# A fused attention and expert kernel: a second buffer for weight conversion, slopes read as rows, block 2's scores behind block 1's transposes, each weight scaling in its own slot

## The chip, the cores and the metric

The kernel runs on one core of a Trainium2 chip. The metric is the time of one execution in device microseconds (us); less is better.

## What is computed

Three stages follow one another. The middle one has the weights that most of the change is about.

```python
# attention: 4 x 8 heads, 576 positions, window of 128, a bias by distance
scores = q @ k.T / sqrt(64) + bias, masked to 0 <= rel < 128
x = softmax(scores) @ v                       # 2304 tokens x 512
# dense layer: w_in 512 x 2048, w_out 2048 x 512, alpha 2048
h = x @ w_in
y = (max(h, 0) + alpha * min(h, 0)) @ w_out
# experts: logits = y @ w_gate; 288 tokens go to each of 8 experts
out[mask] = max(y[mask] @ w1[e], 0) @ w2[e]
```

## The kernel before

The 2304 tokens are 18 blocks of 128. The 8 heads are done in halves, so attention has 36 steps n (block n // 2, half n % 2). The dense layer goes over 9 units u of two blocks and 16 slices f of the hidden dimension: 144 **slots** (u, f), numbered 16 u + f. Slot (u, f) is `l1` (TensorE: `ph`; then two or three operations that make `g`) and, one slot later, `l2` (TensorE: `py`).

`w_in` and `w_out` come as 64-bit numbers, in 16 tiles of 1 MB, one per f. `load_w64` fetches one into `raw` (four buffers), and `split_w64` makes 32-bit numbers of it in `wf`: two operations on ScalarE (L155 writes `w64q`, L160) and three on VectorE (L163 keeps a running maximum `w_top`, L166 and L167 put the bits together). Unit 0 (slots 0 to 15) is computed in 32-bit numbers directly from `wf`, four matmuls of `ph` and two of `py` in a slot. For the other units `w_scales` takes one scale from the maxima of all 16 tiles, and `w_split` makes two 16-bit parts of each tile: `wh` on ScalarE (L211, two operations) and `wl` on VectorE (L212, two).

In unit 0 the path of a slot is `ph` on TensorE, L647 on ScalarE, L648 on VectorE, then `ph` of the next slot, which shares a PSUM tile; beside it L650 on ScalarE and `py` of the slot.

What sets the order: `at(s, fn, ...)` puts the calls in a table by slot number, negative ones before slot 0, and from the program that this writes a scheduler makes one fixed order for each engine. `tc.issue_after(X)` constrains this order: what is in its scope comes after X on X's own engine. On another engine it is seen to have no hold: L211, which stands under `issue_after(TURN[...])` where `TURN` is a VectorE instruction (L648), is found on ScalarE ahead of the slots that it names. All loads but the tiles of `wm` are issued by the queue of SP, as are the first `LF` tiles; the other tiles are issued by ScalarE. Some names: `kr`, `qr` and `vr` are buffers for keys, queries and values, `ks` the keys in two parts (L404 on ScalarE, L405 on GpSimd), `S` the scores (L498), `pt` transposes, `pav` the product with the values, `xf` the attention's result for unit 0 (L613, L618), `vm` the maxima of the values (L418 for block 5, L429 for blocks 1 to 3).

Of the kernel before, what the change touches and what calls it, by code (L numbers as in the profile page):

```python
# [8 lines left out]
F32 = mybir.dt.float32  # L9
# [11 lines left out]
P = 128  # L21
# [6 lines left out]
KG = 25  # L28
WC = 14
WM = 1  # L30
BEHIND = 2
# [3 lines left out]
SH = 0  # L35
SH2 = 0


# [14 lines left out]
GB, CF, XT, ET2 = 2, 4, 7, 8  # L53
LG_, LF, LD = 3, 3, 2
MP0, MP1 = 0, 0
# [19 lines left out]
SP, SE, SS = 0, 8, 0  # L75
WQ = (0, 16, 24)
MX = ()
# [10 lines left out]
def attention_moe_kernel(ctx, tc, qt, kt, vt, wm, alpha, wg, we, out, NB=18, dbg=None):  # L88
# [19 lines left out]
    wf, raw = {}, {}  # L108
    GATE, LOADED, SPLIT, TURN = {}, {}, {}, {}

# [41 lines left out]
    def split_w64_(f):  # L152
        mid, top = raw[f]
        q = mlp.tile([P, 2, 512], U16, name="w64q", tag="yt", bufs=1)
        nc.scalar.activation(q.bitcast(BF16), top.bitcast(BF16), AF.Abs)  # L155
        w = wf[f].rearrange("p (i n) -> p i n", i=2)
        l = w.bitcast(I32)
        upper = wf[f].bitcast(U16).rearrange("p (i n two) -> p i n two", i=2, two=2)[:, :, :, 1]

        SPLIT[f] = nc.scalar.activation(l, q, AF.Relu, bias=least, scale=2.0 ** 19)  # L160
        q = q.bitcast(BF16)
        if f:
            nc.vector.tensor_tensor(w_top, w_top, q, ALU.max)  # L163
        else:
            nc.vector.tensor_copy(w_top, q)
        nc.vector.scalar_tensor_tensor(l, mid, 13, l, op0=ALU.logical_shift_right, op1=ALU.bitwise_or)  # L166
        nc.vector.scalar_tensor_tensor(upper, top, 0x8000, upper, op0=ALU.bitwise_and, op1=ALU.bitwise_or)  # L167
# [33 lines left out]
    def w_split(f):  # L201

        w_parts(f)
        with tc.issue_after(TURN[WC + f - BEHIND].ins):
            w_split_(f)

    def w_split_(f):
        for i, n in enumerate(("in", "out")):
            h = slice(i * 512, (i + 1) * 512)
            sc = WS[n] if n == "in" else WS[n][:, f:f + 1]  # L210
            nc.scalar.activation(wh[f][:, h], wf[f][:, h], AF.Copy, scale=sc)  # L211
            nc.vector.scalar_tensor_tensor(wl[f][:, h], wf[f][:, h], sc, wh[f][:, h], op0=ALU.mult,  # L212
                                           op1=ALU.subtract)

# [20 lines left out]
    slope = [[consts.tile([P, FT], F32, name=f"{n}{i}") for n in ("sg", "sa")] for i in range(2)]  # L235

    def small_loads():
        nc.sync.dma_start(wg_sb, wg.rearrange("(c p) e -> p c e", p=P))
        nc.sync.dma_start(al_sb, alpha.rearrange("(f p) -> p f", p=P))

        (sg, sa), scaled = slope
        nc.vector.tensor_scalar(sg, al_sb, 1.0, -2.0, op0=ALU.is_gt, op1=ALU.mult)
        nc.vector.tensor_scalar(sg, sg, 1.0, None, op0=ALU.add)
        nc.vector.tensor_tensor(sa, sg, al_sb, ALU.mult)
        for a, b in zip(slope[0], scaled):
            nc.vector.tensor_scalar(b, a, 2.0 ** -KG, None, op0=ALU.mult)
# [86 lines left out]
    QR, QH, QL, KR, VP, E, SM, ET, S_, XN = ({} for _ in range(10))  # L333
    XF, XH, XL, MN, VG, VI, VC, XS = {}, {}, {}, {}, {}, {}, {}, {}
    XI = consts.tile([P, NU], F32, name="XI")
    YI = consts.tile([P, NU], F32, name="YI")
# [70 lines left out]
    def prep_v(n):  # L407
        b, hf = divmod(n, 2)
        if hf == 0:

            r = VP.pop((b, "raw"))
            VC[b] = att.tile([P, 8], F32, name="vc", bufs=3)
            pm = VC[b][:, 0:1]
            if b < NV:

                m = att.tile([P, 3], F32, name="vm")
                for i, t in enumerate((VP[b - 2, "all"], VP[b - 1, "all"], r)):
                    nc.vector.tensor_reduce(m[:, i:i + 1], t, axis=AX.X, op=ALU.max, apply_absolute_value=True)  # L418
                nc.vector.tensor_reduce(pm, m, axis=AX.X, op=ALU.max)
            else:  # L420
                nc.vector.tensor_reduce(pm, r, axis=AX.X, op=ALU.max, apply_absolute_value=True)
            VP[b, "pm"] = pm, r

    def unit_scale(b):

        VC[b] = att.tile([P, 8], F32, name="vc", bufs=3)
        m = att.tile([P, 3], F32, name="vm")
        for i in range(3):
            nc.vector.tensor_reduce(m[:, i:i + 1], VP[b - i, "all"], axis=AX.X, op=ALU.max, apply_absolute_value=True)  # L429
# [49 lines left out]
    def a_scores(n, g):  # L479
# [6 lines left out]
        S_[n] = S  # L486
        cut = slice(0, 2) if kind_of(b) != "start" else slice(b % 2, b % 2 + 1)
        if b < NS:
            js = [KPOS[j] for j in ((b,) if kind_of(b) == "start" else (b - b % 2, b - 1 + b % 2))]
# [118 lines left out]
    def a_xt(b):  # L608
# [3 lines left out]
        for c in range(4):  # L612
            nc.tensor.transpose(pt[:, c], xn[:, c * P:(c + 1) * P], ident)  # L613
        cut = slice(i * P, (i + 1) * P)
# [14 lines left out]
    def l1(u, f):  # L629
# [16 lines left out]
        g = mlp.tile([P, 256], F32, name="g", bufs=B1)  # L646
        nc.scalar.activation(g, ph, AF.Copy, scale=sg)  # L647
        TURN[order.index((u, f))] = nc.vector.scalar_tensor_tensor(g, ph, sa, g, op0=ALU.mult, op1=ALU.max)  # L648
# [221 lines left out]
    for u in range(NU):  # L870
# [7 lines left out]
        for i in range(2):  # L878
# [3 lines left out]
            at(s + d + 1, logits, 2 * u + i)  # L882
    at(3 * FT, late_ramps)
    at(GP, gate_parts)
    first = -LEAD - EARLY - 8
# [513 lines left out]
```

## Time and profile before

| | us |
|---|---|
| median of 3 runs | 863.41 (862.65 to 863.48) |
| the profiled execution | 867.34 |
| its span in the trace | 865.6 |

| engine | busy us, share of the span |
|---|---|
| TensorE (PE) | 808.4, 93% |
| weight loads of TensorE (PEld) | 665.4, 77% |
| VectorE (DVE) | 587.5, 68% |
| ScalarE (ACT) | 460.3, 53% |
| GpSimd (POOL) | 280.9, 32% |

Busy shares are means over the whole span, and the stages have different limits; the share that counts is the one in the stage that is changed. A row of the trace has the start of an instruction, its duration, the engine, the line, what it writes and reads, and in brackets how long its engine had stood idle before it and what ended that.

### The profile page before, as it was taken

To read this page: it belongs to the slowest core of one execution; us is meant where nothing else is said; L and a number is where in the kernel's file an instruction comes from. 1 tells how busy PE (TensorE), PEld (TensorE's weight loads), DVE (VectorE), ACT (ScalarE), POOL (GpSimd) and SP (SyncE) were. 2 spreads that over 40 slices of the span, in tenths; PEclk is the share of its full clock that TensorE was granted. 3 is DMA by queue.
4 is the path that set the end of the run, shared out by engine and by line. 5 is a ranking of instruction groups with operands and counts; after the bars stand their busy time and mean duration, and the time that the engine had idled before them with its cause. 6 is when DMAs were issued, how large, how long until landed. Compare 5 with 4: busy or idle time off the path is not lost.

```text
span 865.6 us, 17868 instructions
## 1 busy us (share of the span) xinstructions
PE 808.4 (93%) x6703; PEld 665.4 (77%) x6703; DVE 587.5 (68%) x1762; ACT 460.3 (53%) x1099; POOL 280.9 (32%) x256
## 2 busy tenths in 40 slices
PE   7698879999999999999999999988899989999996
PEld 5576656677777767777777778867899988999996
DVE  7799945998688686887868754476658765753120
ACT  5597674745556555655655444304445553555531
POOL 5242200101110010101100000008678988688921
PEclk9588899999999999999999999968989998999998
DMA  8987401013221122121201000015455555566500
GB/s 246 281 276 242 147 1 36 27 32 95 57 63 49 37 75 61 39 86 50 84 28 37 2 1 26 1 57 188 129 159 190 200 185 148 171 175 201 174 29 27
DMA packets 33765, 88.98 MB, mean 103 GB/s; under 512 B 7440, under 2 KB 7440, under 8 KB 33680
## 3 DMA queue, kind: packets, MB, share of 16 engines
q1 hardware_dynamic: 28736, 64.79, 24.7%
q10 hardware_dynamic: 1872, 13.63, 4.7%
q0 software_dynamic: 3072, 9.44, 3.5%
q8 instruction: 52, 0.85, 0.4%
q14 instruction: 33, 0.27, 0.1%
HBM read 78.40 MB, written 9.44 MB: 101 GB/s over the span
## 4 chain that ended last, share of the span: by engine, by line
PE 74%; DVE 10%; DMA 6%; ACT 4%; POOL 2%; issue 2%; SPq 1%; another core or an unknown queue 0%; POOLq 0%; ACTq 0%; DVEq 0%
PE ph L641 20%; PE py L687 15%; PE pyx L1206 12%; PE phx L1188 10%; PE S L498 3%; PE py L673 2%; DMA kr<-in_k_dram 2%; PE pav L592 2%; DMA wr<-in_we_dram 1%; ACT wp L211 1%; DMA vr<-in_v_dram 1%; PE pav L584 1%; PE prt L989 1%; PE pt L533 1%; DVE wf L167 1%
## 5 line engine op out<-in xcount | busy, mean ns | idle before, releaser
L641 PE MATMUL ph<-xh,wp 128*128 128x256 f16 x1536 | 199.1, 273 | 1.9 <-DVE g L648 1.9
L641 PEld LDWEIGHTS <-wp 128*128 128x128 f16 x1536 | 148.3, 98 | 45.3 <-issue 4.2
L1140 POOL TENSOR_TENSOR ws<-wr,ws 128x512 fp32r<-128x512 f32 x128 | 160.3, 1286 | 18.7 <-ACT ws L1137 18.0
L405 POOL TENSOR_TENSOR ks<-kr,ks 64x512 fp32r<-64x512 f32 x34 | 51.1, 1505 | 297.7 <-ACT ks L404 292.6
L687 PE MATMUL py<-wp,gh 128*128 128x512 f16 x448 | 124.3, 379 | 0.8 <-ACT gh L655 0.8
L647 ACT ACTIVATE g<-ph,sg 128x256 f32<-128x256 f32 x144 | 67.4, 469 | 95.6 <-PE ph L641 94.5
L1206 PE MATMUL pyx<-hh,ws 128*128 128x288 f32 x512 | 111.7, 304 | 0.0
L1137 ACT ACTIVATE ws<-wr 128x512 fp32r<-128x512 f32 x128 | 73.3, 627 | 66.3 <-DMA wr<-in_we_dram 41.4
L648 DVE SCALAR_TENSOR_TENSOR g<-ph,sa,g 128x256 f32<-128x256 f32 x144 | 69.1, 480 | 50.9 <-ACT g L647 50.5
L1188 PE MATMUL phx<-exh,ws 128*128 128x288 f32 x512 | 87.7, 309 | 0.0
L1206 PEld LDWEIGHTS pyx<-hh,ws 128*128 128x128 f32 x512 | 86.0, 192 | 0.0
L655 ACT ACTIVATE gh<-g 128x256 f16<-128x256 f32 x128 | 53.0, 414 | 51.9 <-DVE g L648 46.6
L1188 PEld LDWEIGHTS phx<-exh,ws 128*128 128x128 f32 x512 | 75.7, 196 | 2.1 <-POOL ws L1140 1.5
L1206 PE MATMUL pyx<-hl,ws 128*128 128x288 f32 x256 | 76.4, 298 | 0.0
L687 PE MATMUL py<-wp,gl 128*128 128x512 f16 x224 | 74.2, 380 | 0.0
L656 DVE TENSOR_TENSOR gl<-g,gh 128x256 f16<-128x256 f32 x128 | 55.9, 436 | 18.1 <-ACT gh L655 17.6
L1195 DVE SCALAR_TENSOR_TENSOR hl<-phx,hh 128x288 fp32r<-128x288 f32 x64 | 28.9, 455 | 54.4 <-ACT hh L1194 51.7
L687 PEld LDWEIGHTS <-gh 128*128 128x128 f16 x448 | 42.2, 98 | 29.8 <-ACT gh L655 1.2
L524 ACT ACTIVATE e<-e,mn 128x128 f32<-128x128 f32 x116 | 45.2, 393 | 8.8 <-DVE mn L521 8.6
L1206 PEld LDWEIGHTS pyx<-hl,ws 128*128 128x128 f32 x256 | 49.2, 192 | 0.0
L1194 ACT ACTIVATE hh<-phx 128x288 fp32r<-128x288 f32 x64 | 25.3, 405 | 43.1 <-PE phx L1188 32.5
L1188 PE MATMUL phx<-exl,ws 128*128 128x288 f32 x256 | 47.4, 309 | 0.1
(288 smaller groups left out, 1580.3 us busy)
## 6 DMA issues: line engine op xcount, KB each, us to landing
wr<-in_we_dram SPq DMA_DIRECT2D x64, 512.0 KB, 3.8
raw<-in_wm_dram ACTq DMA_DIRECT2D x13, 1023.8 KB, 7.1
kr<-in_k_dram SPq DMA_DIRECT2D x68, 128.0 KB, 2.8
qr<-in_q_dram SPq DMA_DIRECT2D x64, 128.0 KB, 2.6
y_dram<-y SPq DMA_DIRECT2D x18, 256.0 KB, 2.1
vr<-in_v_dram SPq DMA_DIRECT2D x13, 256.0 KB, 2.7
raw<-in_wm_dram SPq DMA_DIRECT2D x3, 1023.8 KB, 8.2
whole<-in_v_dram SPq DMA_DIRECT2D x4, 256.0 KB, 7.2
```

Of the source, the lines that this page charges most:

```text
L405: nc.gpsimd.tensor_sub(ks[64:], KR[n][64:], f32(ks[64:]))
L524: nc.scalar.activation(e[:, h], e[:, h], AF.Exp, bias=mn[:, h:h + 1], scale=-1.0, accum_out=SM[b][:, hh:hh + 1])
L641: nc.tensor.matmul(ph, w[f][:, c * P:(c + 1) * P], x[u][:, c, :], start=i == 0, stop=i == 4 * len(pairs) - 1)
L647: nc.scalar.activation(g, ph, AF.Copy, scale=sg)
L648: TURN[order.index((u, f))] = nc.vector.scalar_tensor_tensor(g, ph, sa, g, op0=ALU.mult, op1=ALU.max)
L655: nc.scalar.activation(gh, g, AF.Copy)
L656: nc.vector.tensor_sub(gl, g, gh)
L687: nc.tensor.matmul(PY[u][i], a[:, s], w[f][:, 512:], start=f == 0 and j == 0, stop=f == FT - 1 and j == 2)
L1137: nc.scalar.activation(wh[s][:, h], w[:, h], AF.Copy)
L1140: (nc.vector if on_dve else nc.gpsimd).tensor_sub(wl[s][:, h], w[:, h], f32(wh[s][:, h]))
L1188: nc.tensor.matmul(ph, w[s][:, c * P:(c + 1) * P], x[:, c], start=i == 0, stop=i == 11)
L1206: nc.tensor.matmul(py, w[s][:, cs], r[x][f], start=i == 0, stop=i == 23)
```

## The change

Six things are changed.

- `w64q` gets two buffers of its own; before it had one, in a slot of memory that it shared with `yt` and `wgr`.
- `alpha` is read as 16 rows of 128 numbers by the first DMA of SP's queue, and one TensorE transpose brings it into its place; before, one DMA fetched its 2048 numbers one by one. `wg` is read later.
- Four tiles of `wm` go through SP's queue instead of three (`LF`), at other places (`WQ`).
- The scores of steps 4 and 5 (block 2) are put behind the transposes of block 1's result on TensorE.
- The maxima of the values, L429 and L418, are put behind slot 0 and slot 16 on VectorE.
- `w_split` starts at slot 13 instead of 14 (`WC`), and its ScalarE operations are tied to the ScalarE instruction of the slot (`KEPT`, L647), its VectorE operations to the VectorE one (`TURN`).

```diff
-WC = 14
+WC = 13
+SC_ = 0
-LG_, LF, LD = 3, 3, 2
+LG_, LF, LD = 3, 4, 2
-WQ = (0, 16, 24)
+WQ = (0, 14, 22, 26)
...
     def split_w64_(f):
         mid, top = raw[f]
-        q = mlp.tile([P, 2, 512], U16, name="w64q", tag="yt", bufs=1)
+        q = mlp.tile([P, 2, 512], U16, name="w64q", bufs=2)
...
     def w_split(f):
         w_parts(f)
-        with tc.issue_after(TURN[WC + f - BEHIND].ins):
-            w_split_(f)
-
-    def w_split_(f):
         for i, n in enumerate(("in", "out")):
             h = slice(i * 512, (i + 1) * 512)
             sc = WS[n] if n == "in" else WS[n][:, f:f + 1]
-            nc.scalar.activation(wh[f][:, h], wf[f][:, h], AF.Copy, scale=sc)
-            nc.vector.scalar_tensor_tensor(wl[f][:, h], wf[f][:, h], sc, wh[f][:, h], op0=ALU.mult,
-                                           op1=ALU.subtract)
+            with tc.issue_after(KEPT[WC + f - BEHIND].ins):
+                nc.scalar.activation(wh[f][:, h], wf[f][:, h], AF.Copy, scale=sc)
+            with tc.issue_after(TURN[WC + f - BEHIND].ins):
+                nc.vector.scalar_tensor_tensor(wl[f][:, h], wf[f][:, h], sc, wh[f][:, h], op0=ALU.mult,
+                                               op1=ALU.subtract)
...
+    def gate_load():
+        with behind(GP - 10):
+            nc.sync.dma_start(wg_sb, wg.rearrange("(c p) e -> p c e", p=P))
+
+    def behind(t):
+        return tc.issue_after(TURN[t].ins) if t in TURN else nullcontext()
+
+    al_row = consts.tile([FT, P], F32, name="al_row")
+    nc.sync.dma_start(al_row, alpha.rearrange("(f p) -> f p", p=P))
+
     def small_loads():
-        nc.sync.dma_start(wg_sb, wg.rearrange("(c p) e -> p c e", p=P))
-        nc.sync.dma_start(al_sb, alpha.rearrange("(f p) -> p f", p=P))
+        pt = psum.tile([P, FT], F32, name="pr", tag="pt")
+        nc.tensor.transpose(pt, al_row, ident[:FT, :FT])
+        nc.vector.tensor_copy(al_sb, pt)
...
+                with behind(4 * n - LEAD + KV2 - 2):
+                  for i, t in enumerate((VP[b - 2, "all"], VP[b - 1, "all"], r)):
                     nc.vector.tensor_reduce(m[:, i:i + 1], t, axis=AX.X, op=ALU.max, apply_absolute_value=True)
...
+        with behind(SC_):
+          for i in range(3):
             nc.vector.tensor_reduce(m[:, i:i + 1], VP[b - i, "all"], axis=AX.X, op=ALU.max, apply_absolute_value=True)
...
+        with tc.issue_after(XT_[1].ins) if 1 in XT_ and n < 6 else nullcontext():
+            a_scores_(n, g, b, hf, S, cut)
...
-            nc.tensor.transpose(pt[:, c], xn[:, c * P:(c + 1) * P], ident)
+            XT_[b] = nc.tensor.transpose(pt[:, c], xn[:, c * P:(c + 1) * P], ident)
...
-        nc.scalar.activation(g, ph, AF.Copy, scale=sg)
+        KEPT[order.index((u, f))] = nc.scalar.activation(g, ph, AF.Copy, scale=sg)
...
+    at(GP - 8, gate_load)
```

The line numbers of the changed kernel are higher by 10 to 16: L404, L498, L521, L561, L647, L648 and L650 are L414, L514, L537, L577, L663, L664 and L666 there, L211 is L208 and L212 is L210.

How the order of the engines changes is shown at three places. The first is the queue of SP at the start of the program (`whole` holds queries, keys and values of the first blocks). Before:

```order
L238 DMA wg_sb<-in_wg_dram 128x4x8
L239 DMA al_sb<-in_alpha_dram 128x16x1
L140 DMA raw_257<-in_wm_dram 128x4095
L377 DMA kr<-in_k_dram 64x512 x4
L140 DMA raw_336<-in_wm_dram 128x4095
L357 DMA qr<-in_q_dram 64x512 x2
L371 DMA whole_150<-in_v_dram 128x512
```

And in the changed kernel:

```order
L141 DMA raw_235<-in_wm_dram 128x4095
L387 DMA kr<-in_k_dram 64x512 x2
L141 DMA raw_321<-in_wm_dram 128x4095
L387 DMA kr<-in_k_dram 64x512 x2
L141 DMA raw_341<-in_wm_dram 128x4095
L367 DMA qr<-in_q_dram 64x512 x2
L381 DMA whole_152<-in_v_dram 128x512
L367 DMA qr<-in_q_dram 64x512 x2
L381 DMA whole_152<-in_v_dram 128x512
L381 DMA v_626<-in_v_dram 128x512
L237 DMA wg_sb<-in_wg_dram 128x4x8
L381 DMA v_896<-in_v_dram 128x512
```

The two small loads are gone from in front of tile 1, the keys of steps 2 and 3 stand around tile 2, tile 3 is new in this queue, and `wg` stands between two loads of values.

The second place is VectorE in unit 0, where block 4 of the attention has the scores of its second half (step 9) and the masked copies `et` of its first (step 8). Before, between L648 of slot 5 and L648 of slot 6, with the conversion of tiles 12 and 13 in between:

```order
L521 ISA e,mn<-S,sbias 128x128
L521 ISA mn 128x1
L163 TENSOR_TENSOR w_top<-w_top,w64q 128x1024
L561 TENSOR_TENSOR et<-et,t_this 128x512
L167 SCALAR_TENSOR_TENSOR wf_712<-raw_661,wf_712 128x1024
L166 SCALAR_TENSOR_TENSOR wf_712<-raw_692,wf_712 128x1024
L596 TENSOR_SCALAR rc<-sm 128x8
L562 TENSOR_TENSOR et<-et 128x512
L517 COPY_PREDICATED S<-m_prev,S 128x2x128
L648 SCALAR_TENSOR_TENSOR g<-ph,sa_101,g 128x256
```

In the changed kernel the same work stands between slot 9 and slot 10, after all tiles and after `w_scales`:

```order
L537 ISA e,mn<-S,sbias 128x128
L537 ISA mn 128x1
L709 TENSOR_TENSOR YI<-XI,w_s 128x1
L577 TENSOR_TENSOR et<-et,t_this 128x512
L578 TENSOR_TENSOR et<-et 128x512
L612 TENSOR_SCALAR rc<-sm 128x8
L613 RECIPROCAL rc<-rc 128x8
L664 SCALAR_TENSOR_TENSOR g<-ph,sa_101,g 128x256
```

One half step of attention has moved from among the conversions to behind them, by four slots.

The third place is ScalarE behind `w_scales`. Before, the scalings of tiles 0 to 7 stand in front of and around L647 of slot 10:

```order
L211 ACTIVATE wp_1068<-wf_413,w_so 128x512
L211 ACTIVATE wp_1148<-wf_443,w_s 128x512
L211 ACTIVATE wp_1148<-wf_443,w_so 128x512
L211 ACTIVATE wp_1148<-wf_443,w_s 128x512
L211 ACTIVATE wp_1148<-wf_443,w_so 128x512
L211 ACTIVATE wp_1280<-wf_509,w_s 128x512
L211 ACTIVATE wp_1280<-wf_509,w_so 128x512
L647 ACTIVATE g<-ph,sg_100 128x256
L211 ACTIVATE wp_1280<-wf_509,w_s 128x512
L211 ACTIVATE wp_1280<-wf_509,w_so 128x512
```

In the changed kernel there is one pair for each slot, from slot 11 on:

```order
L663 ACTIVATE g<-ph,sg_100 128x256
L208 ACTIVATE wp_964<-wf_370,w_s 128x512
L208 ACTIVATE wp_964<-wf_370,w_so 128x512
L666 ACTIVATE g<-g,sg_100 128x256
L576 ACTIVATE et<-pt 128x512
L540 ACTIVATE e,sm<-e,mn 128x128 x4
L663 ACTIVATE g<-ph,sg_100 128x256
L208 ACTIVATE wp_964<-wf_370,w_s 128x512
L208 ACTIVATE wp_964<-wf_370,w_so 128x512
L666 ACTIVATE g<-g,sg_100 128x256
```

Before, 14 of a run of 16 scalings stood ahead of the instruction of slot 10; now the scalings are pairs that stand between L647 and L650 (now L663 and L666) of their slots.

## Rows read from the trace of the kernel before

**Rows 1.** Windows by stage: busy us of each engine, granted clock, DMA share, GB/s

```profile
0.00:41.60 41.60, 28.28 (x124) 21.71 (x125) 30.73 (x94) 22.83 (x51) 16.63 (x33) 0.71 0.91 266
41.60:107.20 65.60, 56.23 (x267) 44.53 (x267) 61.73 (x117) 52.93 (x107) 21.86 (x15) 0.85 0.72 224
107.20:152.30 45.10, 40.02 (x163) 26.39 (x162) 22.88 (x60) 27.11 (x55) 1.27 (x1) 0.96 0.06 18
152.30:200.00 47.70, 46.55 (x360) 34.86 (x360) 44.53 (x110) 28.92 (x76) 4.61 (x6) 1.00 0.13 40
200.00:865.60 665.60, 637.37 (x5794) 537.85 (x5792) 427.66 (x1385) 328.50 (x812) 236.53 (x201) 0.97 0.29 91
```

**Rows 2.** Chain that ended last, 26 to 162 us: start, duration, what

```profile
26.01 11.90 DMA kr<-in_k_dram
...
40.32 1.88 PE S L498 x7
...
84.22 1.01 PE S L498 x8
...
93.95 2.54 DVE et L561
...
99.02 0.61 DVE et L562
...
161.43 0.44 PE pt L533 x4
```

**Rows 3.** Windows around the small loads: columns as in group 1

```profile
8.00:14.00 6.00, 3.77 (x25) 3.07 (x24) 2.84 (x16) 4.04 (x13) 1.84 (x6) 1.00 0.94 155
14.00:20.00 6.00, 4.21 (x17) 3.26 (x16) 6.00 (x22) 2.84 (x7) 0.61 (x3) 0.79 1.00 319
```

**Rows 4.** Timeline of SP's queue, 5 to 32 us

```profile
6.59 0.53 SPq L239 DMA_DIRECT2D al_sb<-in_alpha_dram  x1
7.16 5.42 SPq L140 DMA_DIRECT2D raw<-in_wm_dram  x1
...
25.50 2.39 SPq L377 DMA_DIRECT2D kr<-in_k_dram  x4
```

**Rows 5.** Timeline of VectorE, 33 to 60 us

```profile
41.58 0.42 DVE L521 CUSTOM_DVE_ANT_0 ew<-S,wb 128x256 f32<-128x256 f32 x1 [2.41 <-PE S L498]
...
49.30 0.42 DVE L521 CUSTOM_DVE_ANT_0 ew<-S,wb 128x256 f32<-128x256 f32 x1 [1.30 <-PE S L498]
...
50.59 0.48 DVE L648 SCALAR_TENSOR_TENSOR g<-ph,sa,g 128x256 f32<-128x256 f32 x1
```

**Rows 6.** Line L429, its three instructions: duration in ns, min/median/max

```profile
L429 DVE TENSOR_REDUCE vm<-whole x3: 668/686/687, 12.8 to 27.9; 128x1 f32<-128x512 f32 x3
```

**Rows 7.** Timeline, 85 to 105 us, attention of block 4 among the conversions

```profile
87.22 1.67 PE L584 MATMUL pav<-whole,spare 128*128 128x64 f32 x14
...
92.64 0.28 DVE L521 CUSTOM_DVE_ANT_0 e<-S,sbias 128x128 f32<-128x128 f32 x1
...
93.49 2.45 POOL L319 TENSOR_TENSOR sbias<-bias,sel 128x1024 bf16<-128x1024 bf16 x1 [5.53 <-DVE mn L521]
...
99.53 0.42 DVE L517 COPY_PREDICATED S<-m_prev,S 128x256 f32<-128x256 uint8 x1
...
103.94 0.68 DVE L391 TENSOR_TENSOR ql<-qr,qh 128x512 fp32r<-128x512 f32 x1
```

**Rows 8.** Timeline, 105 to 160 us, slots 8 to 11

```profile
108.20 1.89 PE L641 MATMUL ph<-xf,wf 128*128 128x256 f32 x8
...
116.59 1.95 ACT L211 ACTIVATE wp<-wf,w_so 128x512 f16<-128x512 f32 x3 [0.36 <-DVE w_so L198]
...
125.66 0.45 ACT L647 ACTIVATE g<-ph,sg 128x256 f32<-128x256 f32 x1
...
126.69 3.68 PE L641 MATMUL ph<-xf,wf 128*128 128x256 f32 x8 [3.97 <-DVE g L648]
```

**Rows 9.** Timeline, 144 to 162 us: slots behind runs of four scalings

```profile
145.52 1.99 PE L641 MATMUL ph<-xf,wf 128*128 128x256 f32 x8 [0.34 <-DVE g L648]
...
153.45 1.47 PE L641 MATMUL ph<-xh,wp 128*128 128x256 f16 x12 [1.19 <-DVE g L648]
```

More of the change, by code (lines that the diff above doesn't have):

```diff
@@ L108, in attention_moe_kernel @@
     wf, raw = {}, {}
-    GATE, LOADED, SPLIT, TURN = {}, {}, {}, {}
+    GATE, LOADED, SPLIT, TURN, KEPT = {}, {}, {}, {}, {}
     def w_whole(f):
@@ L160, in split_w64_ @@
         SPLIT[f] = nc.scalar.activation(l, q, AF.Relu, bias=least, scale=2.0 ** 19)
-        q = q.bitcast(BF16)
         if f:
-            nc.vector.tensor_tensor(w_top, w_top, q, ALU.max)
+            nc.vector.tensor_tensor(w_top, w_top, q.bitcast(BF16), ALU.max)
         else:
-            nc.vector.tensor_copy(w_top, q)
+            nc.vector.tensor_copy(w_top, q.bitcast(BF16))
         nc.vector.scalar_tensor_tensor(l, mid, 13, l, op0=ALU.logical_shift_right, op1=ALU.bitwise_or)
@@ L334, in attention_moe_kernel @@
     XF, XH, XL, MN, VG, VI, VC, XS = {}, {}, {}, {}, {}, {}, {}, {}
+    XT_ = {}
     XI = consts.tile([P, NU], F32, name="XI")
@@ L416, in prep_v @@
                 m = att.tile([P, 3], F32, name="vm")
-                for i, t in enumerate((VP[b - 2, "all"], VP[b - 1, "all"], r)):
+                with behind(4 * n - LEAD + KV2 - 2):
+                  for i, t in enumerate((VP[b - 2, "all"], VP[b - 1, "all"], r)):
                     nc.vector.tensor_reduce(m[:, i:i + 1], t, axis=AX.X, op=ALU.max, apply_absolute_value=True)
@@ L427, in unit_scale @@
         m = att.tile([P, 3], F32, name="vm")
-        for i in range(3):
+        with behind(SC_):
+          for i in range(3):
             nc.vector.tensor_reduce(m[:, i:i + 1], VP[b - i, "all"], axis=AX.X, op=ALU.max, apply_absolute_value=True)
@@ L487, in a_scores, with a_scores_ @@
         cut = slice(0, 2) if kind_of(b) != "start" else slice(b % 2, b % 2 + 1)
+        with tc.issue_after(XT_[1].ins) if 1 in XT_ and n < 6 else nullcontext():
+            a_scores_(n, g, b, hf, S, cut)
+    def a_scores_(n, g, b, hf, S, cut):
         if b < NS:
```

## The prediction

> **What bounds the kernel now.** I read the windows by stage first, because all edits lie in the first 200 us. The reader sees three stages there that differ [rows 1]. Up to 41.6 us no engine is full (VectorE 30.7 us busy) and the DMA engines are (share 0.91). From 41.6 to 107.2 us, from block 2's first score to VectorE's operation of slot 7, VectorE is busy 61.73 of 65.60 us: it converts the tiles, and the slots go at its pace. From 107.2 to 152.3 us, slots 8 to 15, VectorE has only 22.88 us of work and TensorE 40.02 of 45.10. Behind that TensorE is the bound (46.55 of 47.70 us, then 637 of 666), and what it has to do does not change. So the change is worth what it moves the end of unit 0, 152.3 us, plus what it does to unit 1.
>
> Next I read the chain of waits for what starts the VectorE stage: a load of keys on which the chain sits for 11.90 us, then block 2's scores at 40.32 [rows 2]. VectorE stood idle 2.41 us until the first of them, and 1.30 us once more ahead of slot 0 [rows 5]. The windows of the DMA engines show what held this load up: from 8 to 14 us they were as busy as later (share 0.94 against 1.00) but moved 155 GB/s instead of 319 [rows 3]. SP's queue tells why: behind the load of alpha the issue of tile 1 took 5.42 us [rows 4].
>
> The timeline of slots 8 to 11 comes last: from 116.59 on ScalarE ran scalings, L647 of slot 10 had to wait until 125.66 among them, TensorE stood 3.97 us, and the next `ph` took 3.68 us where an undisturbed one takes 1.89 [rows 8].
>
> **The change part by part.** The execution in the trace took 867.34 us, 1.74 outside its span and 3.9 above the median; I sum against it and move the difference to 863.41.
>
> *Small loads and the fourth tile, −2.0 us.* The hole cost (319 − 155) × 6 us = 1.0 MB, 3.1 us at 319 GB/s. The row load of alpha takes an issue slot ahead of everything, up to 0.5 us (the old one took 0.53 [rows 4]); `wg`, 512 of the 2560 small pieces (4 on each partition; alpha has 2048), stays and comes back behind, a fifth of the hole, 0.6 us. That leaves −2.0 for the keys of block 2. The other end is that tile 3, now in SP's queue ahead of these keys, lets the tiles run one further ahead: 1 MB more in front of them is 3.3 us at 319 GB/s, and the keys come 1.3 us later than before. I take −2.0, since a tile from ScalarE's queue was in flight beside them before too. The alpha transpose and copy cost a small operation on each engine beside waits for the first scores: nothing.
>
> The Trainium skill, "DMA: Bandwidth & Descriptors", section "Queues, rings and completion order", says that each DMA engine takes turns between the queues that have work and consumes one queue in order: by it a tile in SP's queue stands in front of the keys, one in ScalarE's only beside them. By the rule alone the term would be nearer to +1.3 than to −2.0, and the sum 3.3 us higher. No row here has both orders.
>
> *Order of block 1's transposes and the second buffer, −1.0 us.* Of the 1.30 us idle ahead of slot 0 [rows 5] I take 1.0 as gone, since the first `ph` no longer stands behind a score that waits, and ScalarE can start a tile while the last one's `w64q` is still read; ends 0 and −1.3.
>
> *Maxima L429, +2.1 us.* Three at 0.69 [rows 6] were done ahead of 41.6 us, where VectorE had idle time; now they stand behind slot 0 in the full stage. L418 leaves the first stage too, where it filled idle time: nothing.
>
> *Attention that leaves the VectorE stage, −4.8 us.* The order shows four scores, L561, L562, two L517, one L391 and the sums' reciprocal behind slot 9 instead of among the conversions. Four scores at 0.28, 1.1; L561 2.54 and L562 0.61 [rows 2]; L517 0.42 each and L391 0.68 [rows 7]. All would be 5.8. But L561 is long because GpSimd works at 93.49 to 95.94 beside it [rows 7]; alone it is like L562, and GpSimd may slow another operation instead: 3.8. I take 4.8, the middle.
>
> VectorE's operation of slot 7 then comes at 107.2 − 2.0 − 1.0 + 2.1 − 4.8 = 101.5, **5.7 us earlier**.
>
> *The scalings, −1.4 us.* With pairs between the slots the wait of 3.97 goes, and the slow `ph` (3.68 − 1.89 = 1.8): −5.8. What was moved out of the stage before must be done here: 8 score matmuls 1.01, four transposes 0.44 [rows 2], 8 matmuls of `pav` 8/14 of 1.67 = 0.95 [rows 7]: +2.4. What is late next is slot 10's VectorE operation, behind 1.1 + 2.54 + 0.61 us of attention, and each slot with a pair on ScalarE. A block of four scalings cost TensorE 0.34 us once and 1.19 the other time [rows 9]; I take 2.0 for all of it (0 to 5).
>
> So unit 0 ends 7.1 us earlier. *Unit 1, +1.0 us.* Twelve more scalings fall into it, 12 × 0.65 (1.95 / 3 [rows 8]) = 7.8 us on ScalarE, which has 28.92 of 47.70 us of work there [rows 1], and the maxima and half a step of attention on VectorE with 44.53. The order shows as much of VectorE's attention pushed on into the next unit, so I take 1.0 (0 to 4). The tie of VectorE's scalings and the load of `wg` behind slot 3 cost nothing: the first was kept before, the second has no hold on SP.
>
> Sum: **−6.1 us**, 861.2 for this execution, 857.3 as a median.
>
> **The rivals.**
>
> *Only the clump goes.* The keys come no earlier (the end of +1.3 above), the idle ahead of slot 0 stays and GpSimd slows another operation: +1.3 + 2.1 − 3.8 = −0.4, then −1.4 and +1.0: −0.8, 862.6. With the keys just as late as before it is −2.1, 861.3. The skill's rule on queues would bring this about. For it: a DMA share of 0.91 over 41 us. Against it: the hole of 1.0 MB, which certainly closes.
>
> *TensorE is never let down.* Slots 8 to 15 follow so closely that no wait is left and the clock stays at its high level (2.4 GHz); the slow `ph` behind the long wait showed the low one (1.2), at 0.96 granted over the stage [rows 1, 8]. Then the 2.0 of waits that I added back and the 1.0 of unit 1 fall away, and two terms reach their better ends (0.3 and 1.0): 4.3 more, 853.0. For it: that stage has 5 us of TensorE's idle time in one place mostly. Against it: VectorE's 4.2 us of attention ahead of slot 10.
>
> *The pairs sit in the path of each slot: slower.* Between L647 and L650 there are now two scalings, 1.3 us, in 16 slots (11 to 26). If `py` and with it the next slot wait for them, all of it is 20.8 us. The gains without this are 7.1 + 2.0 − 1.0 = 8.1, so it decides from 0.5 us a slot on; at one of the two, 16 × 0.65 = 10.4, the kernel ends 2.3 us slower, 865.7. For it: the order shows the pair just there. Against it: four scalings in a row cost 0.34 and 1.19, and ScalarE is idle 18 of 45 us.
>
> *The ties have no hold.* `issue_after` held nothing on another engine before; if it did not here, the clump would stay and only 5.7 − 2.4 − 1.0 = 2.3 us be gained, 861.1. The order shows the pairs in their slots, so this is next to excluded.
>
> **How the numbers follow.** A measurement of this kernel can tell about 0.2%, 1.7 us, from no change. Forecast, 854 to 860.5: 0.54. Only the clump goes, 860.5 to 863.5: 0.20. Never let down, 850 to 854: 0.14. Pairs in the path, 862 to 875: 0.10. Ties without hold, 861.1: 0.02. The first, the third and the last are faster by over 1.7 us, and of the second I count half: 0.54 + 0.14 + 0.02 + 0.10 = 0.80. Slower keeps most of the fourth, 0.09, and 0.11 is left for the same. The range takes in the forecast, most of the closer case and of the clump's: 851.0 to 862.0, which leaves out some 0.15 on the slow side and 0.04 on the other.
>
> **What would show it.** Right: the DMA rate in the window from 8 to 14 us near 300 GB/s; block 2's first score near 38.5 us; VectorE's operation of slot 7 near 101.5; no wait of TensorE above 2 us in slots 8 to 15; the last `py` of unit 0 ending near 145. Wrong: a keys load that lands at 38 us or later, a slot pitch above 5 us in slots 11 to 15, waits of `py` for L650, or low clock in that stage; and unit 1 longer than before by more than 4 us.

## The result and the profile after

The changed kernel takes **855.39 us** (median of 4 runs, 854.78 to 856.74), the kernel before beside it 863.44 (862.65 to 866.35): a ratio of **0.9903**, 95% interval 0.9877 to 0.9929, so 8.05 us less. Forecast were 857.3 and a range of 851.0 to 862.0. The profiled execution took 856.74 us with a span of 855.0; it lies 1.35 above its median, that of before 3.9 above its own, so the two traces differ by 10.6 where the medians differ by 8.05. Disturbed executions are left out, so one variant below has a time but no stages.

The windows of the changed kernel, cut where those of [rows 1] were cut: at block 2's first score, at VectorE's operation of slot 7, at the end of unit 0. The columns are those of [rows 1]: length, busy us of TensorE, of its weight loads, of VectorE, ScalarE and GpSimd (with the count of instructions), granted clock, DMA share, GB/s.

```profile
0.00:44.60 44.60, 28.89 (x129) 21.84 (x130) 33.43 (x90) 22.79 (x53) 16.66 (x32) 0.73 0.85 248
44.60:101.10 56.50, 48.79 (x237) 36.81 (x236) 56.39 (x105) 48.69 (x96) 20.73 (x12) 0.91 0.77 252
101.10:141.80 40.70, 39.46 (x189) 28.13 (x190) 27.88 (x69) 23.00 (x55) 5.76 (x5) 1.00 0.09 26
200.00:855.00 655.00, 627.20 (x5711) 529.27 (x5709) 419.30 (x1360) 321.36 (x795) 234.61 (x200) 0.97 0.30 91
```

| stage | before | after | change | forecast |
|---|---|---|---|---|
| start to block 2's first score | 41.6 | 44.6 | +3.0 | −2.0 |
| to VectorE's operation of slot 7 | 65.6 | 56.5 | −9.1 | −3.7 |
| to the end of unit 0 | 45.1 | 40.7 | −4.4 | −1.4 |
| the rest of the span | 713.3 | 713.2 | −0.1 | +1.0 |

The sum came out near the forecast because errors of both signs met, which is luck: the first stage became longer instead of shorter, the second and third shrank by 8.4 us more than forecast. In the second stage VectorE is busy for 56.39 of 56.50 us, before for 61.73 of 65.60: 5.3 us of work and 3.8 of idle time are gone. In the third, TensorE is busy for 39.46 of 40.70 at a granted clock of 1.00; before it was 40.02 of 45.10 at 0.96.

The hole in the DMA engines' rate [rows 3] closed, as the same two windows show (rate in the last column):

```profile
8.00:14.00 6.00, 3.48 (x18) 3.11 (x18) 4.25 (x24) 4.44 (x18) 1.83 (x6) 0.70 0.99 314
14.00:20.00 6.00, 5.48 (x22) 4.39 (x21) 3.10 (x10) 3.27 (x7) 0.14 (x1) 0.73 1.06 283
```

The keys came later all the same. The timeline of SP's queue, to be held against [rows 4]:

```profile
14.74 4.30 SPq L367 DMA_DIRECT2D qr<-in_q_dram  x2
...
19.72 4.10 SPq L367 DMA_DIRECT2D qr<-in_q_dram  x2
...
28.76 0.39 SPq L237 DMA_DIRECT2D wg_sb<-in_wg_dram  x1
...
31.07 3.56 SPq L387 DMA_DIRECT2D kr<-in_k_dram  x4
```

The keys of step 4 are issued at 31.07 us instead of 25.50 [rows 4], since SP stands among the issues ahead of them: two of `qr` take over 4 us each, and `wg` is issued only at 28.76. From 8 to 45 us the trace puts 13.2 us of SP's waiting down to loads of tiles, that of before 7.3. The chain that ended last then sits 9.59 us on these keys, where it sat 11.90 us on them before [rows 2], so the delay lies in the issue and not behind it:

```profile
31.58 9.59 DMA kr<-in_k_dram
...
43.34 2.09 PE S L514 x8
```

VectorE's timeline has the first score 3.0 us later than [rows 5], but slot 0's operation only 1.7 later (50.59 before), and behind it the three maxima (L441, before L429) that stood in the idle time before [rows 6]:

```profile
44.60 0.43 DVE L537 CUSTOM_DVE_ANT_0 ew<-S,wb 128x256 f32<-128x256 f32 x1 [0.67 <-PE S L514]
...
52.32 0.47 DVE L664 SCALAR_TENSOR_TENSOR g<-ph,sa,g 128x256 f32<-128x256 f32 x1
52.71 1.85 DVE L441 TENSOR_REDUCE vm<-whole 128x1 f32<-128x512 f32 x3
```

Slots 8 to 11 in the timeline. The moved half step of attention stands ahead of slot 10. The waits of `ph` that are left, 0.95 and 0.73 us, are those of slots 8 and 9, ahead of all scalings; the `ph` of slots 10 and 11 (110.36, 115.81) wait for nothing and take 1.89 and 1.95 us, where the one at 126.69 of [rows 8] had waited 3.97 and taken 3.68; the scalings run as a pair behind L663:

```profile
101.60 1.99 PE L657 MATMUL ph<-xf,wf 128*128 128x256 f32 x8 [0.95 <-DVE g L664]
...
106.05 1.99 PE L657 MATMUL ph<-xf,wf 128*128 128x256 f32 x8 [0.73 <-DVE g L664]
...
110.36 1.89 PE L657 MATMUL ph<-xf,wf 128*128 128x256 f32 x8
...
111.48 0.68 DVE L577 TENSOR_TENSOR et<-et,t_this 128x512 f32<-128x512 f32 x1
111.64 2.51 POOL L328 TENSOR_TENSOR sbias<-bias,sel 128x1024 bf16<-128x1024 bf16 x1 [20.70 <-DVE YI L709]
112.20 2.50 DVE L578 TENSOR_TENSOR et<-et 128x512 f32<-128x512 f32 x1
...
115.81 1.95 PE L657 MATMUL ph<-xf,wf 128*128 128x256 f32 x8
...
117.85 0.47 ACT L663 ACTIVATE g<-ph,sg 128x256 f32<-128x256 f32 x1 [0.32 <-PE ph L657]
118.22 0.71 ACT L208 ACTIVATE wp<-wf,w_s 128x512 f16<-128x512 f32 x1
```

Slow beside GpSimd is now L578 (2.50 us), where it was L561 before [rows 2, 7], but it lies in a stage in which VectorE has 13 us to spare.

### The profile page after: what moved, and what is told of

It is laid out like the page before. It is cut to its first block, busy times and chain, and to the rows that moved or that the text cites. A ratio compares the mean times of both kernels' runs of the same rounds, so it can differ in the third digit from the quotient of the medians.

```text
span 855.0 us, 17887 instructions
## 1 busy us (share of the span) xinstructions
PE 800.8 (94%) x6704; PEld 657.5 (77%) x6704; DVE 590.9 (69%) x1763; ACT 458.6 (54%) x1099; POOL 282.6 (33%) x256
## 4 chain that ended last, share of the span: by engine, by line
PE 74%; DVE 12%; DMA 6%; POOL 2%; issue 2%; ACT 2%; SPq 1%; another core or an unknown queue 0%; POOLq 0%; ACTq 0%; DVEq 0%
PE ph L657 20%; PE py L703 15%; PE pyx L1223 12%; PE phx L1205 10%; PE S L514 3%; PE py L689 2%; DMA kr<-in_k_dram 2%; DMA qr<-in_q_dram 2%; PE py L682 2%; PE pav L608 2%; PE prt L1006 1%; DVE wf L167 1%; DVE wf L166 1%; PE pt L549 1%; PE pox L1241 1%
## 5 line engine op out<-in xcount | busy, mean ns | idle before, releaser
L663 ACT ACTIVATE g<-ph,sg 128x256 f32<-128x256 f32 x144 | 67.5, 469 | 98.1 <-PE ph L657 96.2
L664 DVE SCALAR_TENSOR_TENSOR g<-ph,sa,g 128x256 f32<-128x256 f32 x144 | 68.9, 479 | 47.3 <-ACT g L663 47.0
L672 DVE TENSOR_TENSOR gl<-g,gh 128x256 f16<-128x256 f32 x128 | 58.2, 455 | 20.4 <-ACT gh L671 20.1
L540 ACT ACTIVATE e<-e,mn 128x128 f32<-128x128 f32 x116 | 45.1, 392 | 11.0 <-DVE mn L537 10.9
L1211 ACT ACTIVATE hh<-phx 128x288 fp32r<-128x288 f32 x64 | 25.3, 405 | 40.8 <-PE phx L1205 30.3
```

Source lines behind the costliest of these rows:

```text
L540: nc.scalar.activation(e[:, h], e[:, h], AF.Exp, bias=mn[:, h:h + 1], scale=-1.0, accum_out=SM[b][:, hh:hh + 1])
L663: KEPT[order.index((u, f))] = nc.scalar.activation(g, ph, AF.Copy, scale=sg)
L672: nc.vector.tensor_sub(gl, g, gh)
```

## The experiments

The runs fell on several chips, on which the kernel before takes between 855.7 and 863.5 us, so the ratio to the kernel before beside each is what is compared; 0.001 of it is 0.86 us. Differences of 3 us between two ratios are at the edge of what the intervals tell apart. Stages are those of the profiled execution of each: first score, from there to slot 7's VectorE operation, from there to the end of unit 0.

| kernel | ratio, 95% interval | first score | to slot 7 | to the end of unit 0 |
|---|---|---|---|---|
| changed | 0.9903 (0.9877 to 0.9929) | 44.6 | 56.5 | 40.7 |
| changed, again | 0.9913 (0.9886 to 0.9939) | 42.8 | 56.5 | 40.8 |
| scalings as before | 1.0129 (1.0099 to 1.0160) | 43.6 | 60.8 | 51.4 |
| start at 14, new ties | 0.9980 (0.9957 to 1.0004) | 44.1 | 60.4 | 41.4 |
| before, scalings changed | 0.9892 (0.9862 to 0.9923) | 40.8 | 61.6 | 40.9 |
| before, start at 13 | 0.9970 (0.9954 to 0.9987) | 42.2 | 58.7 | 47.6 |
| one buffer | 0.9846 (0.9818 to 0.9875) | 45.4 | 49.7 | 42.4 |
| conversions later | 0.9871 (0.9851 to 0.9891) | 39.9 | 50.7 | 42.2 |
| three tiles | 0.9916 (0.9886 to 0.9947) | 41.2 | 54.5 | 40.8 |
| three tiles, one buffer | 0.9899 (0.9869 to 0.9929) | 43.9 | 49.9 | 42.6 |
| small loads as before | 0.9947 (0.9928 to 0.9966) | 44.8 | 60.1 | 40.8 |
| scores not tied | 0.9941 (0.9918 to 0.9964) | 41.5 | 63.5 | 41.3 |
| maxima early | 0.9903 (0.9872 to 0.9934) | | | |

**The changed kernel again**, unedited.

> The changed kernel once more, beside the others on one chip. Every theory: 0.988 to 0.993 of the kernel before, as measured first (0.9903). It is the base that the variants on the same chip are compared with.

847.97 against 855.66 us, as expected. Two executions of the same code, on two chips, have their first score 1.8 us apart. Three of the variants below keep every engine's order up to the first score as well (scalings as before, start at 14, conversions later), and the five traces have it between 39.9 and 44.6 us; the kernel before and its two variants, with the queue of before, between 40.8 and 42.2. So the +3.0 above is a rough figure, and one execution's first column says little. In this trace it is not the keys that the chain comes through but the transposes of block 1's result, behind which the change ties the scores:

```profile
40.71 1.12 PE pt L629 x4
41.83 1.80 PE S L514 x8
```

**The scalings as before.**

```diff
-WC = 13
+WC = 14
...
-            with tc.issue_after(KEPT[WC + f - BEHIND].ins):
+            with tc.issue_after(TURN[WC + f - BEHIND].ins):
                 nc.scalar.activation(wh[f][:, h], wf[f][:, h], AF.Copy, scale=sc)
```

> The scalings as before (start at slot 14, ScalarE's and VectorE's both tied to the VectorE instruction), all else as in the changed kernel. Theory (the clump was worth 4.4 us, the amount by which slots 8 to 15 became shorter): the run of scalings comes back on ScalarE, one wait of ph for VectorE above 2 us and a ph at the low clock after it; 858.5 to 861. Rival (now that the stage before is shorter, the run of scalings falls where TensorE has other work): no wait of ph above 2 us, 855 to 857.

867.76 against 856.88 us: **slower than before**, by 1.3%. The direction is the theory's, the loss against the changed kernel four times the 4.4 us that it put on the run of scalings. The window from slot 7 to the end of unit 0, and in it the `ph` that waited:

```profile
104.40:155.80 51.40, 45.17 (x175) 31.12 (x176) 23.03 (x56) 27.72 (x59) 3.06 (x3) 0.87 0.07 21
```

```profile
104.90 1.99 PE L657 MATMUL ph<-xf,wf 128*128 128x256 f32 x8 [3.00 <-DVE g L664]
...
112.35 2.77 PE L657 MATMUL ph<-xf,wf 128*128 128x256 f32 x8 [1.98 <-DVE g L664]
...
127.74 3.78 PE L657 MATMUL ph<-xf,wf 128*128 128x256 f32 x8 [3.36 <-DVE g L664]
```

TensorE is let down three times for about 2 us or more instead of once, and the granted clock is 0.87 over the stage, before 0.96. All other edits are in this kernel, and with the old scalings they cost 11 us.

**Start at 14, the new ties kept.**

```diff
-WC = 13
+WC = 14
```

> The changed kernel with WC 14 (the scales and the scalings one slot later), the new ties kept. Theory (the number WC is what puts half a step of attention behind the conversions, the ties only dissolve the run of scalings): the half step stands among the conversions again, slot 7's VectorE operation comes 3 to 4 us later than in the changed kernel, no wait of ph above 2 us, and the kernel is 3 to 6 us slower than the changed one. Rival (the ties carry the whole gain of the scalings): within 1.5 us of the changed kernel.

854.41 against 855.66 us, 6.4 above the changed kernel on the same chip: the theory, a little beyond its 3 to 6, and with one miss. Slot 7 comes at 104.5, and one `ph` does wait:

```profile
105.04 3.78 PE L657 MATMUL ph<-xf,wf 128*128 128x256 f32 x8 [3.02 <-DVE g L664]
```

The half step of attention stands ahead of slot 7 again, the stage to slot 7 is 3.9 us longer, and TensorE waits for it once. With the variant ahead, this splits the scalings on the changed kernel, ties first: the ties are worth 1.0129 − 0.9980, about 13 us, the start at 13 another 6.

**The kernel before with the scalings alone changed**, the diff being to the kernel before.

```diff
-WC = 14
+WC = 13
...
-        with tc.issue_after(TURN[WC + f - BEHIND].ins):
-            w_split_(f)
...
+            with tc.issue_after(KEPT[WC + f - BEHIND].ins):
+                nc.scalar.activation(wh[f][:, h], wf[f][:, h], AF.Copy, scale=sc)
+            with tc.issue_after(TURN[WC + f - BEHIND].ins):
...
-        nc.scalar.activation(g, ph, AF.Copy, scale=sg)
+        KEPT[order.index((u, f))] = nc.scalar.activation(g, ph, AF.Copy, scale=sg)
```

> The kernel before with the scalings alone changed (WC 13 and the new ties), all else as before. Theory (the scalings carry the gain, the other parts together cost time): 8 to 14 us faster than the kernel before, 0.984 to 0.991, as good as the changed kernel or better. Rival (each part gives a share, as the prediction summed them): 2 to 5 us faster than the kernel before, 0.994 to 0.998, and slower than the changed kernel.

847.30 against 855.66 us, 0.9892: **as good as the whole change.** The theory holds, the sum of shares falls. From slot 7 to the end of unit 0 TensorE is busy all but 0.28 us:

```profile
102.40:143.30 40.90, 40.62 (x194) 28.66 (x193) 31.30 (x79) 23.09 (x56) 5.89 (x5) 1.00 0.11 32
```

**The kernel before with the start at 13 alone.**

```diff
-WC = 14
+WC = 13
```

> The kernel before with WC 13 and nothing else; the scalings stay tied as before. Theory (the start at 13 moves half a step of attention out of the full stage by itself, and the run of scalings costs what it did): slot 7's VectorE operation 4 to 6 us earlier than before, a wait of ph above 2 us around slot 10, and 3 to 6 us faster than before, 0.993 to 0.9965. Rival (the run of scalings eats what the move gives, since two half steps of attention now stand in front of slot 10 as well): within 2 us of the kernel before, 0.9975 to 1.0025.

861.21 against 863.50 us, 0.9970, between the two. Slot 7's operation comes at 100.9, 6.3 us earlier than before, a little more than the theory had; but the run of scalings is still there, and TensorE waits five times, 5.0 us in all, once like this:

```profile
119.23 3.58 PE L641 MATMUL ph<-xf,wf 128*128 128x256 f32 x8 [2.20 <-DVE g L648]
```

A half step moved in front of a clump gives back part of what it saved: of the 6.3 us 3.8 are left at the end of unit 0 (148.5 against 152.3), and 2.3 in the medians. With the ties on top the ratio falls to 0.9892, about 7 us: the start brings the work to where there is room, the ties keep TensorE fed there. What either is worth depends on the other: the start gains 6 us with the new ties and 2.3 without them. The traces agree: in every one with the start at 14 block 4's second half has its scores on VectorE ahead of slot 7, in every one with 13 behind it.

**One buffer for `w64q`.**

```diff
-        q = mlp.tile([P, 2, 512], U16, name="w64q", bufs=2)
+        q = mlp.tile([P, 2, 512], U16, name="w64q", tag="yt", bufs=1)
```

> w64q with one buffer in yt's slot again, all else as in the changed kernel. Theory (the second buffer lets the conversions run ahead of half a step of attention, and takes VectorE's idle time away): the half step of block 4 comes back among the conversions, VectorE's stage from the first score to slot 7 takes 62 to 66 us instead of 56.5, and the kernel ends 5 to 9 us later than the changed one, 860 to 864. Rival (the order came from the other edits, and one buffer is freed soon enough): the stage takes 56 to 58 us, 855 to 857.

842.94 against 856.88 us, 0.9846: **the theory fell**, and its rival too. Without the second buffer the changed kernel is faster, by 0.6 to 0.7%; the intervals of both its measurements lie above this one, one of them by a hair, and on other chips. The last operation of a conversion on VectorE, counted up to slot 7's operation, here (95.1 us), in the changed kernel and in the kernel before; and slot 0's here:

```profile
L167 DVE SCALAR_TENSOR_TENSOR wf<-raw,wf x12: 1290/1334/2434, 21.1 to 92.0; 128x1024 uint16<-128x1024 uint16 x12
L167 DVE SCALAR_TENSOR_TENSOR wf<-raw,wf x15: 1285/1329/2404, 21.7 to 99.9; 128x1024 uint16<-128x1024 uint16 x15
L167 DVE SCALAR_TENSOR_TENSOR wf<-raw,wf x15: 1256/1329/2408, 18.7 to 104.5; 128x1024 uint16<-128x1024 uint16 x15
```

```profile
46.12 0.48 DVE L664 SCALAR_TENSOR_TENSOR g<-ph,sa,g 128x256 f32<-128x256 f32 x1
```

Twelve tiles are converted ahead of slot 7, not 15 as in the changed kernel, and slot 0 comes at 46.12 instead of 52.32. The reading that I take from it: a second buffer in itself only takes a wait away; what costs is the order that the scheduler writes with it. The kernel before converts 15 tiles ahead of slot 7 with one buffer, so the number of buffers alone does not set this order, and no run gives the kernel before a second one.

**Two buffers, conversions held back.** It tests that reading with both buffers kept.

```diff
-WL = 6
+WL = 4
```

> The changed kernel, two buffers and all, with WL 4 instead of 6: from slot 3 on the conversion of a tile is held two slots longer, so that 13 tiles instead of 15 are converted ahead of slot 7's VectorE operation, and the rest stand one to a slot up to slot 10. Theory (one buffer was faster because the conversions run less far ahead of the slots): slot 7's operation comes 5 to 7 us earlier than in the changed kernel, unit 0 ends 3 to 5 us earlier, and the time is 3 to 5 us below the changed kernel, 0.985 to 0.988 of the kernel before. Rival (one buffer was faster by the early slot 0 alone, the later conversions only wait in another place): unit 0 ends within 1.5 us of the changed kernel, 0.989 to 0.993.

851.37 against 863.50 us, 0.9871, inside what the theory gave, outside the rival's. The stage to slot 7 is nearly as short as with one buffer, with 13 conversions ahead of slot 7. The interval still overlaps that of the changed kernel, so it is the stages that speak for this reading, not yet the time. The profiled execution was the shortest of five (846.84, median 851.37), and its first score at 39.9 is 2.9 us ahead of the changed kernel's earliest with the same order up to there; that part is not the edit's. VectorE's work in the stage, 49.58 against 56.39, is.

```profile
39.90:90.60 50.70, 46.96 (x237) 35.21 (x236) 49.58 (x99) 47.03 (x94) 20.07 (x12) 0.95 0.86 279
90.60:132.80 42.20, 39.99 (x189) 28.16 (x190) 33.57 (x74) 24.74 (x56) 6.67 (x5) 1.00 0.09 26
```

VectorE is full in the first of these windows (49.58 of 50.70) and has 33.57 of 42.20 in the second, 5.7 more than in the changed kernel: conversions went to where TensorE is the bound.

**Three tiles in SP's queue.**

```diff
-LG_, LF, LD = 3, 4, 2
+LG_, LF, LD = 3, 3, 2
-WQ = (0, 14, 22, 26)
+WQ = (0, 16, 24)
```

> Three tiles in SP's queue again (LF 3, WQ as before), all else as in the changed kernel. Theory (the fourth tile stands ahead of block 2's keys): the load of the keys of step 4 is issued by 26 us instead of 31.07, block 2's first score on VectorE comes near 39 to 41 us instead of 44.60, and the kernel ends 2 to 4 us earlier than the changed one, 851.5 to 853.5. Rival (the early tiles are what shortens the VectorE stage): the score comes earlier all the same, but VectorE then waits for tile 3 or later ones; slot 7's VectorE operation stays at 101 us or later and the time is 855 to 858.

849.07 against 856.88 us, 0.9916. The mechanism is the theory's, as SP's queue and VectorE show:

```profile
25.21 2.39 SPq L387 DMA_DIRECT2D kr<-in_k_dram  x4
```

```profile
41.18 0.42 DVE L537 CUSTOM_DVE_ANT_0 ew<-S,wb 128x256 f32<-128x256 f32 x1 [0.97 <-PE S L514]
```

The fourth tile does delay the keys, by 5.9 us at their issue in these two traces: the five traces with three tiles have it between 25.2 and 26.5 us, the eight with four that have stages in the table between 27.4 and 31.2. The keys are there at 35.4, 2.6 us earlier than before, but the first score gains only 0.4, as slot 0's `ph` now runs ahead of the scores on TensorE:

```profile
36.55 3.78 PE L657 MATMUL ph<-xf,wf 128*128 128x256 f32 x8 [1.13 <-ACT xf L634]
```

The time does not follow either: it is that of the changed kernel. The profiled execution, in which unit 0 ends at 136.5, was the shortest of six (843.31; the others up to 851.53), so its stages do not stand for the others. Why they are longer stays open.

**Three tiles and one buffer.**

```diff
-LG_, LF, LD = 3, 4, 2
+LG_, LF, LD = 3, 3, 2
...
-        q = mlp.tile([P, 2, 512], U16, name="w64q", bufs=2)
+        q = mlp.tile([P, 2, 512], U16, name="w64q", tag="yt", bufs=1)
```

> The changed kernel with three tiles in SP's queue and with one buffer for w64q: both parts undone. Theory (the late keys and the second buffer each cost time for themselves): unit 0 ends 7 to 11 us earlier than in the changed kernel, and the time is 6 to 10 us below it. Rival (both only delay slot 0's ph, so either of them undone takes away the same time): unit 0 ends 4 to 6 us earlier, and the time is 4 to 6 us below the changed kernel, no better than with one buffer alone.

846.15 against 855.66 us, 0.9899: the two gains do not add up, as the rival had it, but against it little is left of the gain with one buffer (1.8 us to the changed kernel on the same chip). With three tiles one buffer or two makes no difference that the intervals tell (0.9899, 0.9916). The profiled execution was the shortest here too (843.58 of up to 850.17). Open as well.

**The small loads as before** (`alpha` number by number, `wg` in front of tile 1).

```diff
-    al_row = consts.tile([FT, P], F32, name="al_row")
-    nc.sync.dma_start(al_row, alpha.rearrange("(f p) -> f p", p=P))
...
-        nc.tensor.transpose(pt, al_row, ident[:FT, :FT])
-        nc.vector.tensor_copy(al_sb, pt)
+        nc.sync.dma_start(wg_sb, wg.rearrange("(c p) e -> p c e", p=P))
+        nc.sync.dma_start(al_sb, alpha.rearrange("(f p) -> p f", p=P))
...
-    at(GP - 8, gate_load)
```

> alpha number by number and wg in front of tile 1 again, all else as in the changed kernel (four tiles in SP's queue). Theory (the hole in the DMA engines' rate delays the keys on top of the fourth tile): 150 to 170 GB/s from 8 to 14 us, the keys' first score 2 to 3 us later than in the changed kernel, near 47 us, and 857 to 858.5. Rival (the queue's order alone sets when the keys come, the hole falls into time in which nothing is waited for): first score near 44.6 us, 854.5 to 856.

852.32 against 856.88 us, 0.9947: 3 to 4 us slower than the changed kernel, near the size of the theory, though the intervals touch. Its way there was wrong. The hole is back (173 GB/s from 8 to 14 us), yet the first score is at 44.8 and the keys are issued at 29.47, no later than with the row load. What comes late, as I read it, are the tiles: between 40 and 66 us ScalarE waits 3.3 us for them (0.5 and 1.2 in the two traces of the changed kernel), and in the stage to slot 7 VectorE stands once for 3.9 us behind ScalarE.

```profile
ACT w64q L156 <- DMA raw<-in_wm_dram: 3.3, 3, 2.0
```

```profile
DVE g L661 <- ACT g L660: 3.9, 1, 3.9
```

**The scores of block 2 not tied.**

```diff
-        with tc.issue_after(XT_[1].ins) if 1 in XT_ and n < 6 else nullcontext():
+        with nullcontext():
```

> The changed kernel with the scores of block 2 free to stand ahead of block 1's transposes; the ph of slot 0 then stands behind all scores of steps 4 and 5. Theory (VectorE's work ahead of slot 7 is the same, so an early slot 0 is worth little): slot 0's VectorE operation 2 to 4 us later, slot 7's within 1 us of the changed kernel, the time within 1.5 us of it. Rival (what slot 0 loses, all slots lose): slot 7 also 2 to 4 us later, and the time 2 to 4 us above the changed kernel.

858.50 against 863.50 us, 0.9941, some 3 us above the changed kernel (the intervals overlap), by the rival: slot 7 comes at 105.0. Slot 0's operation comes at 53.31, only 1.0 us later, against both. VectorE's work in the stage is the same, 56.75 us, but the stage is 63.5 long: idle time is back, 6.7 us of it, more than the 3.87 of before.

```profile
41.50:105.00 63.50, 50.53 (x236) 37.48 (x235) 56.75 (x106) 50.24 (x97) 16.83 (x12) 0.88 0.70 226
```

**The maxima early.**

```diff
-                with behind(4 * n - LEAD + KV2 - 2):
+                with nullcontext():
...
-        with behind(SC_):
+        with nullcontext():
```

> The changed kernel with the maxima of the values (L429 and L441) where the scheduler puts them by itself, ahead of slot 0. Theory (they were done in idle time, and cost 1.9 us in the full stage): slot 7's VectorE operation 1.5 to 2.5 us earlier than in the changed kernel and the time 1 to 2.5 us below it. Rival (ahead of slot 0 they stand in front of the scores, and cost the same there): within 1 us of the changed kernel.

855.85 against 863.50 us, with a ratio of 0.9903, the changed kernel's own: the rival. Where the maxima stand makes no difference that this shows.

## Why the prediction was right, and where it was not

*The bound of each stage* was read rightly: VectorE up to slot 7, TensorE behind, and the forecast of slot 7's operation (101.5) met 101.08. It did so by luck, by terms whose errors cancelled.

*Small loads and the fourth tile, −2.0; measured +3.0 at the first score.* The step that failed is "I take −2.0, since a tile from ScalarE's queue was in flight beside them before too". In flight beside is not the same as ahead in the queue: with the tile in SP's queue the keys were issued 5.6 us later, without it at 25.21. The rule of the Trainium skill, "DMA: Bandwidth & Descriptors", section "Queues, rings and completion order", that was set against it gave the right sign; by it the term was +1.3. What the traces show is a later issue by SP; once issued the keys took no longer to land than before (9.59 us against 11.90), so what the rule says of the DMA engines themselves is not tested here. The term also left out the path from the keys to the score: the tie puts the scores behind block 1's transposes, which held them in the changed kernel again, and without the tie the first score is at 41.5 with four tiles. A sign of being wrong that the prediction had set did come, keys that land behind 38 us (41.2). The rate of 314 GB/s was forecast rightly and is worth some 3 us, but not through the keys; that it is through the tiles is a reading of one trace.

*Order of block 1's transposes and the second buffer, −1.0.* Two things in one term. The order is worth more: I took only the 1.30 us ahead of slot 0 [rows 5], though the window showed 65.60 − 61.73 = 3.87 us of idle time in the stage [rows 1]. They are gone (0.11 left), and without the tie 6.7 are there. The buffer has the other sign in the changed kernel: it costs some 5 us there, with three tiles nothing that the intervals tell.

*Maxima, +2.1*: 1.85 us of VectorE, near what was put, but undoing it gains nothing that can be measured.

*Attention that leaves the VectorE stage, −4.8*: VectorE's work fell by 5.3 us although the maxima came in, so 7.2 left, above the upper end of 5.8. The conversions in the stage take 40.3 us in both traces, so it is attention that left. What moves the half step is the number 13, which I had not named: with 14 the stage to slot 7 is 3.9 us longer.

*The scalings, −1.4; measured −4.4.* The failing step is the 2.0 us "for all of it", the new waits behind the pairs: they did not come, no `ph` of slots 10 to 15 waits. TensorE's idle time in the stage fell from 5.1 to 1.2 us, more than the one wait of 3.97, and its busy time stayed (40.02, now 39.46), the slow `ph` gone against the moved work. In this stage the rival "TensorE is never let down" was right, with a granted clock of 1.00, though not in its time of 853.0. The slower rival, pairs in the path of each slot, did not show: no `py` waited for L666. One sign of it that I had set was badly chosen: the operations of slots 12 to 14 do stand more than 5 us apart (123.55 to 128.75 to 134.24), because TensorE is full there (16.00 of the 16.00 us from 118.3 on), not because it waits.

*Unit 1, +1.0*: from slot 16's to slot 36's VectorE operation it takes 67.3 instead of 64.7 us, 2.6 more. The three L429 (L418 before) stand ahead of slot 17:

```profile
141.11 0.68 DVE L429 TENSOR_REDUCE vm<-whole 128x1 f32<-128x512 f32 x1
...
142.89 0.48 DVE L664 SCALAR_TENSOR_TENSOR g<-ph,sa,g 128x256 f32<-128x256 f32 x1
```

Over the rest of the span nothing of it is left, −0.1 us, but that is within what two executions differ by.

*As a whole:* the gain was forecast as a sum of parts, and the runs show that it is one part. The scalings alone give it all (0.9892); the other parts seem to gain some (the order of the scores and the small loads, some 3 us each, with intervals that touch) and to lose as much (the second buffer), and with the old scalings their sum is a loss, 1.0129.

**The best kernel seen** is the changed one with a single buffer, 0.9846: 1.5% below the kernel before, and below the changed one. Why it loses that with three tiles is open.

## What to carry to other kernels

Ahead of the point where the bound moves from one engine to another, the first engine should do only what the next slots need; what can wait, conversions for later slots included, belongs behind; the half step of attention shows it by its times, the conversions so far by their stages and one time. Look at the order that a scheduler writes with a relaxed constraint before counting a second buffer as a gain. For a load in SP's queue, count what SP has to issue ahead of it, not what is in flight beside.

## What was not expected of the hardware

A wait of about 3 us does not always cost TensorE its clock: with the scalings as before a `ph` that had waited 3.00 us took 1.99, and one that had waited 1.98 took 2.77; with the start at 14 one that had waited 3.02 took 3.78. The granted clock in the three, third from last in the rows, was 1.00, 0.69 and 0.50 (1.00 is 2.4 GHz; the first two rows are of the scalings as before, the last of the start at 14):

```profile
104.90:106.90 2.00, 2.00 (x9) 1.79 (x10) 2.00 (x3) 1.48 (x4) 0.79 (x1) 1.00 0.00 0
112.35:115.12 2.77, 2.77 (x9) 2.21 (x10) 0.09 (x2) 0.49 (x1) 0.00 (x0) 0.69 0.00 0
105.04:108.82 3.78, 3.78 (x9) 3.06 (x10) 3.78 (x5) 0.85 (x2) 2.21 (x1) 0.50 0.00 0
```

So the cost of a wait is not read from its length alone.

Executions of one kernel on one chip differ by up to 10 us (maxima early: 849.75 to 859.74, at granted clocks of 0.965 and 0.954; three tiles: 843.31 to 851.53, at 0.971 and 0.958), and which of them is profiled is chance. A stage of one trace is a mechanism, not yet a gain.
